# Gates of batch 0 in one Softplus pass, masks first, later v loads and a new written-out order in a gated linear attention with an MLP mixer

## Chip, cores and metric

The kernel runs on one core of a Trainium2 chip. The metric is the device time of one execution in microseconds (us); the median of several executions counts. Engines: PE (TensorE, matrix products), DVE (VectorE), ACT (ScalarE), POOL (GpSimd), SP (SyncE, here only for DMA), and 16 DMA engines that serve all queues.

## What is computed

```python
f = 1.0 / (1.0 + np.exp(-f_logit))              # B, H, S, D = 4, 8, 768, 48
for t in range(S):
    state = f[:, :, t, :, None] * state + np.einsum('bhd,bhe->bhde', k[:, :, t], v[:, :, t])
    y[:, :, t] = np.einsum('bhd,bhde->bhe', q[:, :, t], state)
x = y.transpose(0, 2, 1, 3).reshape(B, S, H * D)        # 768 x 384 for each batch
h = np.maximum(x.transpose(0, 2, 1) @ w_tok1, 0.0) @ w_tok2
u = x + h.transpose(0, 2, 1)
out = u + np.maximum(u @ w_ch1, 0.0) @ w_ch2
```

## The kernel before

**Attention.** A batch is worked in three chunk pairs, P 0 to 2, each of 256 steps: two chunks of 128 partitions in all, two steps (j) for each partition. For a pair, ACT makes the negative logarithm of the gate from f in place, ln(1 + exp(-f)), in two passes over 128x768 (`gates`, L449 with Exp and L451 with Ln). The pair sum `two` adds the two steps (L444, by the helper `both`); PE multiplies it with the triangular matrix `tri` to running sums (L473; for later batches L475 and L476 in bf16) and, in batch 0, with `ones` to chunk totals (L480, into the same bank of PSUM). `first` (DVE, L502) takes the second step off. From sums and `first` ACT makes the decays GG with four Exp passes (L505, L522) and the totals' decay `glast` (L508; L512 for later batches, moved by a DMA, L518). DVE multiplies q and k with them (L444, tile qk, one product for each j). PE turns the result over `ident` (L550; two PSUM banks), ACT and DVE copy it out as qT and kT (L430, L432); in batches 2 and 3 the DMA does the turn (L535). Then come the scores (L585), masked to AmT by DVE (L628), or by ACT and POOL in four cases of batch 0 (L623, L625); the states' sums (L603), scaled by `glast` (L637) and copied to `state_bd`; and the outputs y from AmT and v (L669) and from q and the state (L661). y goes to x_bf and x_nat.

**Mixer.** tok1 (L713) and, after Relu to h1T, tok2 (L729) work over the steps; u_bf takes y plus the result, is turned (L770; by DMA, L759, for late batches) to uT. ch1 (L788) makes 2 x 12 groups of three products, evacuated by Relu to zT (ACT L439, DVE L441). ch2 (L807) adds twelve products for a tile of 128 rows; DVE adds u (L813), SP stores it (L706). The last tile of the last batch is split in 288 and 96 columns.

**What sets the order.** Nothing runs as it is written: `add` notes each operation with what it needs and makes, and `Plan.best` goes through a written-out list, `ORDER`, in which each number names an operation (by 4) and its choice of engine (mod 4). A model of costs (`cost`, `SLOTS`, `HELD`) gives each a start, and the operations are issued sorted by these starts. So each engine has a fixed order, and engines and queues work strictly in it. Where the model sees PE idle, it sets **empty products** (`idle`, L848: 128x512 over a constant tile, `steady`, that nothing reads). The model's numbers are no times of this profile.

**Loads.** f of batch 0 comes over SP and ACT, all other loads over POOL's queue; a load of POOL waits until the eighth before it has landed.

Of the kernel before, what the change touches and what calls it, by code (L numbers as in the profile page):

```python
# [79 lines left out]
)  # L80
KEPT = 3
EARLY = ()
SPLIT = ()
MASKED = ((0, 0, 1), (1, 0, 1), (1, 1, 1), (2, 0, 1))
SLOTS = (6000, 7500, 10200, 11300, 12500, 13700, 14800, 16000, 17100, 20100, 21900)
HELD = (4300, 4300, 7100)


class Op:
# [167 lines left out]
def kernel(  # L257
# [25 lines left out]
    def st(shape, dtype, tag):  # L283
        return sb.tile(shape, dtype, tag=tag, name=tag)
# [597 lines left out]
```

## Time and profile before

| | |
|---|---|
| three runs | 168.51, 168.56, 169.04 us (median 168.56) |
| profiled execution | 168.51 us, span 166.8 us from the first to the last instruction |
| busy | PE 158.5, DVE 129.3, ACT 106.0, POOL 63.5 us |
| empty products | 32, 10.3 us of PE's busy time |
| chain that ended last | PE 75%, ACT 13%, DVE 5% of the span |
| moved | HBM read 25.17 MB, written 4.72 MB |

A row of the timeline gives start and length in us, engine, line, operation, output<-inputs, shapes and xcount; in brackets stands the idle time of the engine before it, and what ended it. "issue" means that it waited for nothing that the profile shows. A q behind the engine's name is its queue. A row of DMA issues gives the count, the size and the time from issue to landing.

### The profile page before, as it was taken

The numbers are of one execution on the slowest core, as the hardware profiler recorded it, in microseconds if no ns is written. First come the engines' busy times: TensorE is split into PE (matmuls) and PEld (weight loads), VectorE is DVE, ScalarE is ACT, GpSimd is POOL, SyncE is SP. The second block draws the span as 40 slices with busy tenths as digits, with TensorE's granted clock in tenths as the row PEclk, the third lists the DMA queues.
The fourth block names the chain that finished last, engine by engine and source line by source line (L and its number), as shares of the span: only waits on it lengthen the run. The fifth ranks groups of instructions, "written<-read, shape, count | busy, mean of one in ns | idle before, by whom it ended". The sixth has DMA issues, their size and how long they took to land.

```text
span 166.8 us, 5023 instructions
## 1 busy us (share of the span) xinstructions
PE 158.5 (95%) x2064; PEld 101.5 (61%) x2064; DVE 129.3 (78%) x287; ACT 106.0 (64%) x228; POOL 63.5 (38%) x87
## 2 busy tenths in 40 slices
PE   5899997899999999999999999999999999999991
PEld 2467865656666666566665766665667566566660
DVE  3499995889899998999999998996699446460331
ACT  3788975789899999976957939386531311725000
POOL 7975899705877200675517003024022022000000
PEclk9999999999999999999999999999999999999998
DMA  5999999999999991599999660985730043600253
GB/s 122 220 177 171 202 211 238 190 233 217 207 221 217 224 238 27 77 162 198 198 199 141 125 165 0 106 158 118 185 120 4 0 98 81 205 0 4 78 194 105
DMA packets 68183, 24.34 MB, mean 146 GB/s; under 512 B 60896, under 2 KB 67296, under 8 KB 68160
## 3 DMA queue, kind: packets, MB, share of 16 engines
q0 software_dynamic: 41856, 13.77, 67.6%
q1 hardware_dynamic: 25776, 10.06, 28.2%
q8 instruction: 16, 0.26, 0.6%
q10 hardware_dynamic: 528, 0.20, 0.4%
q14 instruction: 7, 0.06, 0.1%
HBM read 25.17 MB, written 4.72 MB: 179 GB/s over the span
## 4 chain that ended last, share of the span: by engine, by line
PE 75%; ACT 13%; DVE 5%; issue 2%; DMA 2%; DVEq 0%; ACTq 0%
PE ps L788 27%; PE ps L807 22%; PE ps L729 4%; PE ps L713 4%; PE ps L585 3%; PE ps L669 3%; ACT state_bd L430 2%; PE ps L661 2%; DMA f_sb<-in_f_logit_dram 2%; PE ps L603 2%; ACT f_sb L449 2%; ACT GG L522 2%; PE ps L550 2%; ACT f_sb L451 2%; ACT GG L505 1%
## 5 line engine op out<-in xcount | busy, mean ns | idle before, releaser
L807 PE MATMUL ps<-w_ch,zT 128*128 128x384 bf16 (+2 forms) x300 | 52.1, 320 | 0.4 <-ACT x_nat L430 0.4
L788 PE MATMUL ps<-uT,w_ch 128*128 128x384 bf16 x288 | 50.3, 326 | 0.1
L807 PEld LDWEIGHTS <-zT 128*128 128x128 bf16 x300 | 28.2, 98 | 17.7 <-issue 0.4
L788 PEld LDWEIGHTS <-w_ch 128*128 128x128 bf16 x288 | 27.7, 98 | 17.9 <-issue 0.3
L439 ACT ACTIVATE zT<-ps 128x384 bf16<-128x384 f32 x58 | 26.0, 495 | 16.9 <-PE ps L788 16.7
L628 DVE TENSOR_TENSOR AmT<-ps,mask 128x512 bf16<-128x512 f32 x44 | 28.3, 680 | 1.0 <-PE ps L585 0.8
L441 DVE TENSOR_SCALAR zT<-ps 128x384 bf16<-128x384 f32 x38 | 20.0, 552 | 6.1 <-PE ps L788 6.0
L813 DVE TENSOR_TENSOR x_nat<-x_nat,ps 128x384 f32<-128x384 f32 (+2 forms) x25 | 13.0, 532 | 10.3 <-PE ps L807 10.3
L434 POOL CAST state_bd<-state 48x192 bf16<-48x192 f32 x16 | 5.9, 369 | 33.0 <-DVE state L645 24.3
L444 DVE TENSOR_TENSOR qk<-qk_sb,GG 128x768 bf16<-128x768 bf16 x24 | 13.9, 585 | 1.2 <-ACT GG L522 1.1
L745 DVE TENSOR_TENSOR x_nat<-x_nat,ps 128x384 f32<-128x384 f32 x21 | 10.6, 548 | 3.9 <-PE ps L729 3.9
L358 POOL DMA_DIRECT2D v_sb<-in_v_dram x12 | 10.7, 888 | 5.7 <-DMA w_ch<-in_moe_w_ch_dram 4.9
L505 ACT ACTIVATE GG<-ps 128x384 bf16<-128x384 f32 x24 | 10.8, 488 | 3.1 <-DVE first L502 1.4
L522 ACT ACTIVATE GG<-first 128x384 bf16<-128x384 f32 x24 | 11.8, 520 | 0.6 <-DVE first L502 0.4
L449 ACT ACTIVATE f_sb<-f_sb 128x768 f32<-128x768 f32 x12 | 10.1, 845 | 2.9 <-DMA f_sb<-in_f_logit_dram 2.9
L848 PE MATMUL ps<-steady 128*128 128x512 bf16 x32 | 10.3, 444 | 1.7 <-DVE steady L373 1.7
L434 POOL COPY qT<-qJ 128x1024 bf16<-128x1024 bf16 x5 | 6.0, 1197 | 14.7 <-DMA qJ<-qk 14.6
L358 POOL DMA_DIRECT2D qk_sb<-in_k_dram x12 | 10.8, 900 | 2.0 <-POOLq L866 0.8
L430 ACT ACTIVATE u_bf<-x_nat 128x384 bf16<-128x384 f32 x13 | 6.0, 528 | 8.0 <-DVE x_nat L745 8.0
L358 POOL DMA_DIRECT2D qk_sb<-in_q_dram x12 | 10.6, 887 | 1.3 <-DMA qk_sb<-in_q_dram 0.7
L430 ACT ACTIVATE x_bf<-ps 128x384 bf16<-128x384 f32 x13 | 6.3, 490 | 6.2 <-PE ps L669 4.4
L713 PE MATMUL ps<-x_bf,w_tok 128*128 128x384 bf16 x48 | 10.1, 326 | 0.1
(84 smaller groups left out, 227.8 us busy)
## 6 DMA issues: line engine op xcount, KB each, us to landing
out_dram<-x_nat SPq DMA_DIRECT2D x23, 192.0 KB, 2.2
f_sb<-in_f_logit_dram POOLq DMA_DIRECT2D x9, 384.0 KB, 8.6
qk_sb<-in_k_dram POOLq DMA_DIRECT2D x12, 192.0 KB, 8.7
qk_sb<-in_q_dram POOLq DMA_DIRECT2D x12, 192.0 KB, 8.7
v_sb<-in_v_dram POOLq DMA_DIRECT2D x12, 192.0 KB, 8.8
w_ch<-in_moe_w_ch_dram POOLq DMA_DIRECT2D x2, 576.0 KB, 13.9
w_ch<-in_moe_w_ch_dram POOLq DMA_DIRECT2D x1, 1152.0 KB, 13.1
f_sb<-in_f_logit_dram SPq DMA_DIRECT2D x2, 384.0 KB, 5.6
```

Of the source, the lines that this page charges most:

```text
L358: lambda eng=eng, into=held(dst[i], P), of=runs(src, b, P): eng.dma_start(out=into, in_=of),
L430: nc.scalar.activation(out_, in_, AF.Copy, bias=0.0, scale=1.0)
L439: nc.scalar.activation(out_, in_, AF.Relu, bias=0.0, scale=1.0)
L441: nc.vector.tensor_scalar(out_, in_, 0.0, None, ALU.max)
L444: (nc.vector if op.engine == DVE else nc.gpsimd).tensor_tensor(out_, a, b_, what)
L449: add(ACT, r, lambda: nc.scalar.activation(fb, fb, AF.Exp, bias=0.0, scale=-1.0), make=[key], kind=el, need=([("fb", P)] if P < 1 else []) ...
L522: add(ACT, r, lambda n=n: nc.scalar.activation(GG[i][:, 0, n], banks[p_f.at][:, 0:DM].rearrange("t (h d) -> t h d", d=D) if split else fir ...
L628: add(DVE, r, lambda into=into, made=made, m4=m4: nc.vector.tensor_tensor(into, made(), m4, ALU.mult), need=masks, make=[("AmT", i, js, pa ...
L713: add(PE, rank("tok1", rt), lambda rt=rt, kt=kt, pm=pm: nc.tensor.matmul(banks[pm.at][:, 0:DM], lhsT=w_tok1[:, kt, rt * 128:(rt + 1) * 128 ...
L788: nc.tensor.matmul(banks[pm.at][:, 0:384], lhsT=w[:, kt, c0:c0 + 128], rhs=uT[:, th, :, kt, :], start=(kt == 0), stop=(kt == 2))
L807: nc.tensor.matmul(banks[pm.at][:, 0:n1 - n0], lhsT=zT[:, kt, tt * 128:(tt + 1) * 128], rhs=w_ch2[:, kt, n0:n1], start=(kt == 0), stop=(kt ...
L813: add(DVE, rank("ch2", tt), lambda un=un, pm=pm, n=n1 - n0: nc.vector.tensor_tensor(un, un, banks[pm.at][:, 0:n], ALU.add), make=[("x_nat" ...
```

## The change

1. **One pass.** In P 0 and P 1 of batch 0 (`SOFT`) the gate is one ACTIVATE with Softplus. ACT starts with the table set "softplus" and loads the one with Exp and Ln behind these two passes; everything of batch 0 that uses Exp waits for it ("tables").
2. **Masks first.** DVE sets all constants in one operation at the start (`constants`), and the first pair sum waits for `ident` and `tri2`. `steady` is a single column now, read as a broadcast. `tri_less` and two unused variants go.
3. **Totals of P 0** go to the bank of the states (p_st) instead of that of the sums.
4. **Loads.** v of P 1 stands behind q and k of P 2 (`LOADS`).
5. **Empty products** get margins: fewer are set into a gap.
6. **Costs** of the model are changed, the last tile's 288 columns go ahead of its 96 (`closing`), and `ORDER` is new as a whole, with other choices of engine.

The new numbering of lines is that of the diff; products with `steady` go from 32 to 22. Three places show what moves. Names carry the number of the buffer (GG_82 and GG_83 are the two decay tiles of even and odd pairs).

ACT, from its first pass on, before (batch 0: passes of P 0 and P 1, decays, then P 2):

```order
L449 ACTIVATE f_sb_74<-f_sb_74 128x8x96
L451 ACTIVATE f_sb_74<-f_sb_74 128x8x96
L449 ACTIVATE f_sb_74<-f_sb_74 128x8x96
L451 ACTIVATE f_sb_74<-f_sb_74 128x8x96
L505 ACTIVATE GG_82<-ps_121 128x384 x2
L522 ACTIVATE GG_82<-first_80 128x384 x2
L508 ACTIVATE glast_94<-ps_121 128x4x2
L505 ACTIVATE GG_83<-ps_122 128x384
L449 ACTIVATE f_sb_74<-f_sb_74 128x8x96
L451 ACTIVATE f_sb_74<-f_sb_74 128x8x96
L430 ACTIVATE qT_86<-ps_124 128x1024
L505 ACTIVATE GG_83<-ps_122 128x384
```

After:

```order
L452 ACTIVATE f_sb_74<-f_sb_74 128x8x96 x2
L839 ACT_TABLE_LOAD
L500 ACTIVATE GG_82<-ps_120 128x384
L517 ACTIVATE GG_82<-first_80 128x384 x2
L500 ACTIVATE GG_82<-ps_120 128x384
L500 ACTIVATE GG_83<-ps_121 128x384 x2
L503 ACTIVATE glast_94<-ps_122 128x4x2
L455 ACTIVATE f_sb_74<-f_sb_74 128x8x96
L432 ACTIVATE qT_86<-ps_123 128x1024
L457 ACTIVATE f_sb_74<-f_sb_74 128x8x96
L503 ACTIVATE glast_95<-ps_121 128x4x2
L517 ACTIVATE GG_83<-first_81 128x384 x2
```

Two passes stand where four stood, a table load behind them; the second decays of P 1 now stand ahead of Exp of P 2 and of qT.

DVE at the mixer of batch 0, before, from the second half of h1T to the third copy to uT:

```order
L441 TENSOR_SCALAR h1T<-ps_122 128x384
L432 CAST u_bf<-ps_127 128x384
L745 TENSOR_TENSOR u_bf<-x_nat_104,ps_121 128x384
L745 TENSOR_TENSOR u_bf<-x_nat_104,ps_123 128x384
L745 TENSOR_TENSOR u_bf<-x_nat_104,ps_128 128x384
L432 COPY uT<-ps_125 128x3x128
L745 TENSOR_TENSOR x_nat_104<-x_nat_104,ps_123 128x384
L432 COPY uT<-ps_126 128x3x128
L745 TENSOR_TENSOR x_nat_104<-x_nat_104,ps_121 128x384
L432 COPY uT<-ps_125 128x3x128
```

After, from the first copy to u_bf at the same place:

```order
L434 CAST u_bf<-ps_120 128x384
L739 TENSOR_TENSOR u_bf<-x_nat_104,ps_121 128x384
L434 COPY uT<-ps_127 128x3x128
L434 COPY uT<-ps_125 128x3x128
L434 COPY x_nat_104<-ps_124 128x384
L739 TENSOR_TENSOR u_bf<-x_nat_104,ps_126 128x384
L739 TENSOR_TENSOR u_bf<-x_nat_104,ps_122 128x384
L739 TENSOR_TENSOR x_nat_104<-x_nat_104,ps_126 128x384
L739 TENSOR_TENSOR x_nat_104<-x_nat_104,ps_122 128x384
L446 TENSOR_TENSOR two_77<-f_sb_75 128x8x48
L739 TENSOR_TENSOR x_nat_104<-x_nat_104,ps_121 128x384
```

h1T is ACT's alone, and uT copies stand ahead of two of the three sums to u_bf.

POOL's queue from its sixth load on (k, q and v of a pair are three rows; qk_sb_68 and v_sb_71 are batch 0's, 69 and 72 batch 1's), before:

```order
L358 DMA v_sb_71<-in_v_dram 128x8x96
L358 DMA qk_sb_68<-in_k_dram 128x8x96
L358 DMA qk_sb_68<-in_q_dram 128x8x96
L358 DMA v_sb_71<-in_v_dram 128x8x96
L403 DMA w_tok_63<-in_moe_w_tok_dram 128x6x256
L365 DMA w_tok_64<-in_moe_w_tok_dram 128x2x768
L365 DMA w_ch_65<-in_moe_w_ch_dram 128x3x768
L365 DMA w_ch_66<-in_moe_w_ch_dram 128x3x768
L358 DMA f_sb_75<-in_f_logit_dram 128x8x96
L625 TENSOR_TENSOR AmT_92<-AmT_92,mask 128x512
L358 DMA qk_sb_69<-in_k_dram 128x8x96
L358 DMA qk_sb_69<-in_q_dram 128x8x96
```

After, from the same load on:

```order
L356 DMA qk_sb_68<-in_k_dram 128x8x96
L446 TENSOR_TENSOR two_77<-f_sb_74 128x8x48
L356 DMA qk_sb_68<-in_q_dram 128x8x96
L356 DMA v_sb_71<-in_v_dram 128x8x96 x2
L416 DMA w_tok_63<-in_moe_w_tok_dram 128x6x256
L363 DMA w_tok_64<-in_moe_w_tok_dram 128x2x768
L363 DMA w_ch_65<-in_moe_w_ch_dram 128x3x768
L363 DMA w_ch_66<-in_moe_w_ch_dram 128x3x768
L446 TENSOR_TENSOR qk_85<-qk_sb_68,GG_83 128x2x8x48
L619 TENSOR_TENSOR AmT_92<-AmT_92,mask 128x512
L446 TENSOR_TENSOR qk_84<-qk_sb_68,GG_82 128x2x8x48
L356 DMA f_sb_75<-in_f_logit_dram 128x8x96
```

The pair sum of P 1 and one half each of the products with q and k of P 1 and P 2 have come to POOL from DVE, and batch 1's loads stand behind the last two.

The diff, cut to its core:

```diff
-    8, 12, 0, 20, 24, 28, 4, 16, 244, 248, 252, 256, 140, 32, 44, 48, 36, 168, 120, 124, 132, 172, 40, 268, 128,
...
+    0, 4, 12, 16, 8, 20, 24, 28, 32, 188, 192, 196, 80, 88, 92, 96, 100, 357, 104, 108, 48, 36, 40, 44, 52, 56,
...
-EARLY = ()
-SPLIT = ()
+SOFT = (0, 1)
+LOADS = (("v", 0), ("kq", 1), ("kq", 2), ("v", 1), ("v", 2))
-SLOTS = (6000, 7500, 10200, 11300, 12500, 13700, 14800, 16000, 17100, 20100, 21900)
-HELD = (4300, 4300, 7100)
+SLOTS = (6150, 7850, 10350, 11500, 12700, 13850, 15000, 16450, 17400, 19500, 21800)
+HELD = (3850, 4300, 7100)
...
-            if e == PE and free[PE] < until and t - free[PE] > 250:
-                n = int((t - free[PE] - 1000) / 430) if not free[PE] else int((t - free[PE] - 40) / 218)
+            if e == PE and free[PE] < until and t - free[PE] > 270:
+                n = int((t - free[PE] - 500) / 430) if not free[PE] else int((t - free[PE] - 50) / 215)
...
-    steady = st([128, 512], BF16, "steady")
+    steady = st([128, 1], BF16, "steady")
...
+    nc.vector.memset(steady, 1.0)
     nc.vector.memset(tri_bf, 1.0)
-    nc.vector.memset(steady, 1.0)
+
+    def constants():
+        nc.vector.memset(ones, 0.0)
...
+    once(DVE, constants, ["ones", "start"] + [(n, i) for n in ("two", "ends") for i in range(2)] + [("sbd", i) for i in range(3)]
+         + [("qk", i, j) for i in range(NQ) for j in range(2)], 2550)
...
-    once(ACT, lambda: nc.scalar.preload_act_table_set("natural_log_exp_and_others"), ["table"], 1280)
+    once(ACT, lambda: nc.scalar.preload_act_table_set("softplus" if SOFT else "natural_log_exp_and_others"), ["table"], 1280)
...
-    load("v", 0, 0)
-    load("kqv", 0, 1)
-    load("kqv", 0, 2)
+    for what, P in LOADS:
+        load(what, 0, P)
...
+        if b == 0 and P in SOFT:
+            add(ACT, r, lambda: nc.scalar.activation(fb, fb, AF.Softplus, bias=0.0, scale=-1.0), make=[key, ("soft", P)], kind=el,
+                need=["table"] + ([("fb", P)] if P < 1 else []))
+            return
...
-        op = add((DVE, POOL) if b == 0 else DVE, r, None, need=[key], make=[("two", i)], kind=("el", DM, False, 1.2))
+        op = add((DVE, POOL) if b == 0 else DVE, r, None, need=[key] + (["ident", "tri2"] if b + P == 0 else []), make=[("two", i)], kind=("el", DM, False, 1.2))
...
+        p_n = p_st if P == 0 else p_s
+        n0 = HP * D if P == 0 else DM
...
-                nc.tensor.matmul(banks[p_s.at][:, DM + 2 * hp:DM + 2 * hp + 2], lhsT=blk(two[i])[:, hp, :], rhs=ones,
-                                 start=True, stop=True)
...
+                nc.tensor.matmul(banks[p_n.at][:, n0 + 2 * hp:n0 + 2 * hp + 2], lhsT=blk(two[i])[:, hp, :], rhs=ones,
+                                 start=P > 0 or hp == 0, stop=True, skip_group_check=P == 0)
...
+                    if b == B - 1:
+                        if n0:
+                            plan.ops[-1].before.update(closing)
+                        else:
+                            closing.append(plan.ops[-1])
...
+            if b == 0 and P == len(SOFT):
+                once(ACT, lambda: nc.scalar.preload_act_table_set("natural_log_exp_and_others"), ["tables"], 1280 if SOFT else 10,
+                     ["table"] + [("soft", p) for p in SOFT])
...
-            nc.tensor.matmul(banks[NBANK - 1], lhsT=steady[:, 0:128], rhs=steady, start=True, stop=True)
+            nc.tensor.matmul(banks[NBANK - 1], lhsT=steady.broadcast_to((128, 128)), rhs=steady.broadcast_to((128, 512)), start=True, stop=True)
```

More of the change, by code (lines that the diff above doesn't have):

```diff
@@ L162, in cost @@
         if what == "el":
-            free, psum, fast = n
+            free, psum, fast, *more = n
             if engine == ACT:
@@ L167, in cost @@
             if engine == DVE:
-                own = free / (0.96 * int(fast)) + 67
-                return own, own + 83
+                own = free / (0.96 * int(fast)) + 67 + sum(more)
+                return own, own + 83 - sum(more)
             own = free * (2.05 if fast % 1 else 1.2) + 80
@@ L464, in sums_and_turns @@
         p_s = Bank()
-        early, split = b == 0 and P in EARLY, b == 0 and P in SPLIT
+        p_n = p_st if P == 0 else p_s
+        n0 = HP * D if P == 0 else DM
         def sums():
             pm = banks[p_s.at][:, 0:DM]
-            if early:
-                for j in range(2):
-                    nc.tensor.matmul(pm, lhsT=tri, rhs=fb[:, :, j], start=j == 0, stop=j == 1)
-            elif b == 0:
+            if b == 0:
                 nc.tensor.matmul(pm, lhsT=tri, rhs=two[i][:, :, 0:D], start=True, stop=True)
@@ L609, in attention @@
         if b:
-            chain = add(PE, r, lambda: parts(range(live)), need=have, bank=p_d[0], kind=("mm", 450 if live > 1 else 260), tail_of=chain)
+            chain = add(PE, r, lambda: parts(range(live)), need=have, bank=p_d[0], kind=("mm", 352), tail_of=chain)
             plan.maker[p_d[live - 1]] = chain
@@ L635, in attention @@
             if b == 0:
-                add(PE, r, lambda x=x: parts([x]), need=have, make=["sums"], bank=p_st, kind=("mm", 300))
+                add(PE, r, lambda x=x: parts([x]), need=have, make=["sums"], bank=p_st, kind=("mm", 365))
                 add(DVE, r, lambda x=x, gb=gb: nc.vector.tensor_tensor(dg(x), dg(x), gb, ALU.mult),
@@ L683, in attention @@
         lead = add(PE, r, lambda: None, need=ready, bank=p_y[0], kind=("mm", 1), room=2)
[L684 removed]
+        lead = add(PE, r, outs, need=ready, bank=p_y[1], kind=("mm", 775 if P else 510), tail_of=lead)
         plan.maker[p_y[0]] = lead
[L686 removed]
+        add(PE, r, lambda: before(1, False), need=past(1), bank=p_y[1], kind=("mm", 200))
         for x in range(2):
```

85 lines of the change are left out of this document (36 added, 49 removed), and 109 rows, old and new, of the table ORDER.

## Prediction

> **What bounds the kernel now.** I read the page first, then the table by stretches of 10 us.
>
> ```profile
> PE   5899997899999999999999999999999999999991
> ...
> PEclk9999999999999999999999999999999999999998
> ...
> L848 PE MATMUL ps<-steady 128*128 128x512 bf16 x32 | 10.3, 444 | 1.7 <-DVE steady L373 1.7
> ...
> 30.00:40.00 10.00, 9.57 (x72) 6.06 (x70) 9.20 (x21) 9.31 (x22) 4.17 (x6) 1.00 1.52 214
> 40.00:50.00 10.00, 10.00 (x143) 6.85 (x142) 9.44 (x20) 9.47 (x20) 7.55 (x9) 1.00 1.84 215
> 50.00:60.00 10.00, 9.57 (x191) 6.70 (x190) 9.80 (x22) 9.98 (x22) 4.42 (x6) 1.00 1.81 225
> 60.00:70.00 10.00, 9.81 (x138) 6.17 (x137) 9.51 (x21) 9.83 (x24) 1.61 (x2) 1.00 0.54 91
> ```
>
> The first two rows of digits cut the span in 40 slices (busy share and granted clock, in tenths). In the stretches, behind the bounds and the length, stand the busy times of PE, PEld, DVE, ACT and POOL. From 32 us on, PE is busy almost without a break; between 30 and 70 its idle time is 0.43 + 0.43 + 0.19 us. So behind the start **TensorE is the bound**: the same products take the same time in whatever order, and only what comes ahead of that stage and behind it can shrink. Ahead of it PE only looks busy: 32 empty products (L848, 10.3 us) fill its waits. There the chain runs f, gates, decays, products with q and k, turns, scores, three chunk pairs one behind the other, and then the mixer of batch 0. PE becomes the bound with the first ch1 product at 32.77. So the time is about: start of ch1, plus PE's remaining work, plus the tail. From 40 to 70 ACT is just as full (29.3 of 30 us), which makes the first rival.
>
> **The start.** Rows of the opening, in order of time:
>
> ```profile
> 1.32 1.28 ACT L376 ACT_TABLE_LOAD   x1 [1.32 <-PEq L866]
> ...
> 4.43 0.84 ACT L449 ACTIVATE f_sb<-f_sb 128x768 f32<-128x768 f32 x1 [1.82 <-DMA f_sb<-in_f_logit_dram]
> ...
> 3.30 0.31 POOL L380 TENSOR_SCALAR_AFFINE_SELECT tri_bf<-tri_bf 128x128 bf16<-128x128 bf16 x1
> ...
> 6.21 0.90 POOL L358 DMA_DIRECT2D v_sb<-in_v_dram  x1
> ...
> 6.79 0.91 PE L473 MATMUL ps<-two,tri 128*128 128x384 f32 x2 [0.43 <-DVE two L444]
> ...
> 7.54 0.95 PE L480 MATMUL ps<-ones,two 128*128 128x2 f32 x8
> ...
> 8.53 0.56 DVE L502 TENSOR_TENSOR first<-ps,f_sb 128x384 f32<-128x384 f32 x1 [0.18 <-PE ps L480]
> ...
> 9.12 0.87 ACT L505 ACTIVATE GG<-ps 128x384 bf16<-128x384 f32 x2 [1.37 <-DVE first L502]
> ...
> 9.87 0.94 ACT L522 ACTIVATE GG<-first 128x384 bf16<-128x384 f32 x2
> ...
> 11.32 0.49 DVE L444 TENSOR_TENSOR qk<-qk_sb,GG 128x768 bf16<-128x768 bf16 x1
> ...
> 12.23 1.07 PE L550 MATMUL ps<-ident,qk 128*128 128x128 bf16 x16
> ...
> f_sb<-in_f_logit_dram SPq DMA_DIRECT2D x1, 384.0 KB, 4.2
> ```
>
> Before, f of P 0 takes two ACT passes (L449, L451), and `first` waits until 8.53 for the totals (L480), since they write the bank that it reads. After, one pass is enough: 4.43 + 0.84 = 5.27. Then the pair sum (0.56, as `first`) and the sums (0.91): 6.8. The second pass can't start before f of P 1 has landed (the last row: issued at 1.35, 4.2 us later, 5.6), so it ends at 6.46, and the new table load (1.28) at 7.75. The decays need table and sums: 7.77, against 9.12. Four of them took 1.69 (9.12 to 10.81), so they end at 9.46, and the products with q and k (0.55 each) at 10.2, against 11.81. Now PE is late: the pair sum of P 1 is on POOL, behind its sixth load, so it starts at about 7.1 (where the sixth, L358 of v, ends now). No row shows it there; by elements from POOL's own product below (1.27 for 512) it takes 0.95, bounded by DVE's 0.56 and by 1.27. I take 0.9: 8.0. Sums (0.75 till the next starts), two totals (0.8 each) and an empty product follow: the turns start at 10.65, a **gain of 1.6 us** over 12.23.
>
> It does not last:
>
> ```profile
> 14.63 0.48 PEld L585 LDWEIGHTS <-kT 48*64 48x64 bf16 x32 [0.27 <-DVE kT L432]
> ...
> 16.30 0.55 DVE L444 TENSOR_TENSOR qk<-qk_sb,GG 128x768 bf16<-128x768 bf16 x1
> ...
> 16.59 1.27 POOL L625 TENSOR_TENSOR AmT<-AmT,mask 128x512 bf16<-128x512 bf16 x1 [0.93 <-ACT AmT L623]
> ...
> 19.55 0.71 PE L585 MATMUL ps<-qT,kT 48*64 48x128 bf16 x32
> ...
> 22.68 0.64 PE L585 MATMUL ps<-qT,kT 48*64 48x128 bf16 x32
> ```
>
> *Scores of P 0*: on ACT, qT stands behind the decay of the totals (which end at 10.5) and Exp of P 2 (0.84), so it starts at 11.6; with 1.02 for itself the scores come at 12.7 against 14.63, gain 1.9. *P 1*: half of the product with q and k is now POOL's. From 512 elements in 1.27 its 768 take 1.7 to 1.9 (bounds: DVE's 0.55, and 1.9), and it waits for the last decays, which stand on ACT behind qT and Ln of P 2 and end at 14.4 (11.6 + 0.9 + 0.9 + 0.94, by starts): 14.4 to 16.2, against 16.85. Then ACT's order has two state copies ahead of qT: scores at 18.85, against 19.55, gain 0.7. *P 2*: DVE's half waits for the decays from `first`, 19.6; turns at 20.25, and qT, behind an AmT copy, x_nat and two state copies, ends at 22.66: scores at 22.7, **no gain** over 22.68. The passes saved on ACT return as waits for the next chunk's decays; the three products that went to POOL spare DVE 3 x 0.55, which is not what ends last there.
>
> **The mixer of batch 0.**
>
> ```profile
> 26.02 0.32 PE L669 MATMUL ps<-v_sb,AmT 64*128 64x48 bf16 x11 [1.09 <-issue]
> ...
> 28.61 0.49 ACT L439 ACTIVATE h1T<-ps 128x384 bf16<-128x384 f32 x1 [0.51 <-PE ps L713]
> ...
> 29.10 0.56 DVE L441 TENSOR_SCALAR h1T<-ps 128x384 bf16<-128x384 f32 x1 [1.04 <-PE ps L713]
> ...
> 30.07 0.87 ACT L430 ACTIVATE u_bf<-ps 128x384 bf16<-128x384 f32 x2 [0.97 <-PE ps L729]
> ...
> 31.17 0.67 PE L770 MATMUL ps<-ident,u_bf 128*128 128x128 bf16 x9
> ...
> 32.12 0.35 DVE L432 COPY uT<-ps 128x384 bf16<-128x384 bf16 x1
> ...
> 32.26 0.68 PE L770 MATMUL ps<-ident,u_bf 128*128 128x128 bf16 x9 [0.43 <-DVE u_bf L745]
> ...
> 32.77 1.46 PE L788 MATMUL ps<-uT,w_ch 128*128 128x384 bf16 x8
> ...
> q8 instruction: 16, 0.26, 0.6%
> ```
>
> PE stands for 1.09 us in the middle of L669 and waits for nothing that the profile shows. Page part 3 has 16 packets of 16 KB on the instruction queue; I read this wait as such a block that came late. PE's 20 rows less move the place by ten products, to the end of the same group, and the block is asked for some 0.4 us earlier, since the scores of P 1 end earlier by that and more: the wait ends at 25.6. The Trainium skill, Runtime: NRT & Kernel Launch, section Instruction fetch mechanics, says that the instructions come in blocks of 16 KiB and that the cost of crossing into the next one is mostly hidden; by that the sum would be the one of the last rival below. The row of L669 shows 1.09 us that were not hidden.
>
> From there: eight L661 and P 2's 32 L669 end at 26.5, a copy of y on DVE (0.56) at 27.4, and the last two tok1 products (0.163 each, and some 0.2 to the end) at 28.0, where h1T starts (28.61). Both halves are ACT's, so the second ends at 28.9 instead of 29.66. The sixth tok2 product, with which three tiles are ready, ends at 29.5, ACT's two u_bf (0.87) at 30.3, and nine transposes start there (31.17). ch1 stands behind these nine alone; before, it stood behind 18, with 0.43 of waiting between. The uT copies (0.35 on DVE, the last behind the ninth transpose) are covered in part by two tok2 products, so ch1 starts at **31.1, 1.67 earlier**. Nine transposes (0.67 busy, 0.5 on PE's queue) are only moved behind it. Net gain: 1.67 - 0.50 = 1.17.
>
> **The tail.**
>
> ```profile
> 156.65 0.25 DVE L813 TENSOR_TENSOR x_nat<-x_nat,ps 128x96 f32<-128x96 f32 x1 [1.77 <-PE ps L807]
> ...
> 163.22 0.55 DVE L813 TENSOR_TENSOR x_nat<-x_nat,ps 128x384 f32<-128x384 f32 x1 [0.78 <-PE ps L807]
> ...
> out_dram<-x_nat SPq DMA_DIRECT2D x1, 192.0 KB, 1.9
> out_dram<-x_nat SPq DMA_DIRECT2D x1, 48.0 KB, 1.5
> ```
>
> The last tile is now the one of 96 columns: behind PE's last product stand 0.25 instead of 0.55, and a store that lands 1.5 instead of 1.9 us behind its issue (the row with 192 KB is the last store alone). The full tile ahead of it ends at almost the same time (its sum is free 12 short products earlier, and its store is longer), so I count 0.55 of these 0.7.
>
> **Sum**, from the profiled execution's 168.51 (span 166.8, 1.7 around it; the median of the runs is 168.56): 168.51 - 1.17 - 0.55 = 166.8. At nothing I cost, first, the masks ahead of the first pair sum, which now waits for two of them: DVE's five small copies follow POOL's select (3.61) and end by about 4.8, 0.5 ahead of f's pass, and even a later sum is covered until the table has come at 7.75. Then v behind q: scores need q and k alone. Then `steady` in one column: 11 empty products at their mean of 0.444 end at 6.0, where the sums begin, and 0.9 us more would be covered by the table load. Last, the loads behind POOL's products:
>
> ```profile
> 25.27 1.06 POOL L365 DMA_DIRECT2D w_ch<-in_moe_w_ch_dram  x1
> ...
> w_ch<-in_moe_w_ch_dram POOLq DMA_DIRECT2D x1, 1152.0 KB, 13.1
> ```
>
> w_ch2 lands at 38.4. After, it is issued some 2 us later, but it lands when the loads ahead of it have passed, and the first ch2 product stands behind 51 ch1 products (0.163 each, from 8 in 1.46 less the last's end) and a few turns: about 40. Later than that, each microsecond would be one of PE's.
>
> **Rivals.** *ACT gives the gain back.* In 40 to 70 ACT has 0.72 us to spare, and the same evacuations are asked for some 1.2 us earlier. For it: 9.98 of 10. Against it: PE waited only 0.43 for all that. Then the tail alone remains, and half a microsecond of the front at most: 168.0, around the border between faster and the same (about 0.3%, 0.5 us, is what a measurement of this kernel can tell from no change).
>
> *Slower, by the same place:* ACT's queue is in order. If the new order sets one chunk of batch 1 so that PE meets its scores before ACT has passed four decays (1.69) and qT (0.92), PE stands for 2.6 us: 169.4. It decides from 2.3 us of such waits on. PE's order is wholly new from ch1 on, with the first ch2 products some 200 rows earlier; this speaks for it.
>
> *The clock falls back.* Empty products go from 32 to 22, and between 5 and 13 us PE will be idle for about 2 us in pieces of 0.4 to 1. The granted clock is 9 or more in every slice but the last, and the pause of 1.09 us did not change it; but no row shows so thin a stretch of 8 us. At half the clock, what PE does for P 0 until its turns end (two sums 1.5, totals 1.6, turns 0.9) takes 4 us more on the path: 170.8. It decides from 2.3 us on. A one-column operand that feeds PE more slowly would end here too.
>
> *The table change costs more.* The first load took 1.28, but nothing was under way ahead of it. If the same 1.28 is paid once more behind the passes of P 0 and P 1, decays start at 9.05; the turns, then bound by ACT, at 11.6, and ch1 some 0.9 later: 167.7. The Trainium skill, ScalarE: Activation LUTs, section What ACT_TABLE_LOAD costs, gives 1283 ns for the load and 1380 ns of drain, 2.66 us for each switch. By it this case would come out 0.1 us later than priced here. The first load's row agrees with the 1283 ns; no row shows a drain, since ACT was idle ahead of it.
>
> *The block wait is gone.* If the block comes in time, the group of P 2 behind it waits for DVE's last AmT instead, ready at about 25.1, and PE gains 0.8 us: 166.0. Against it: loads fill the queues at that place as before.
>
> **How the numbers follow.** Forecast (166.1 to 167.5) 0.45; no block wait 0.12; dearer table 0.06; ACT gives back 0.17 (0.07 of it faster, 0.10 the same); a chunk of batch 1 late 0.13; clock 0.07. Faster: 0.45 + 0.12 + 0.06 + 0.07 = 0.70; the same 0.10; slower 0.20. The likeliest gives 166.8. The range goes from the case without the block wait and 0.6 us less of waiting in the full stage (of the 1.05 us of idle time between 30 and 70) to the late chunk: 165.4 to 169.4.
>
> **What will show it.** In the changed profile: a second table load of 1.28 that ends near 7.75, decays at 7.8, turns of P 0 at 10.65; scores near 12.7, 18.9 and 22.7; a wait of PE without a releaser near 24.6 to 25.6; ch1 near 31.1; PE idle by no more than some 1 us between there and the last product; a last row of 96 columns on DVE. If scores of P 2 come before 22, the loss on ACT was overrated; if ch1 is early and the time is not, one of the first two rivals holds, and PE's waits for ACT between 40 and 70 name the row. The prediction is wrong if PE's idle time behind ch1 grows by over 1 us, or if ch1 comes later than 32.

## The result, and the profile after

The changed kernel takes **167.01 us** (median of 20 runs, 166.45 to 171.42), the kernel before 168.61 in the same comparison: a ratio of 0.9906, 95% interval 0.9882 to 0.993. Ratios here and below leave out runs that took over 1.5% longer than the fastest run of their kernel. The forecast was 166.8. The profiled execution took 167.46, 1.05 less than the 168.51 of before. First its two rows of digits, busy share of PE and granted clock:

```profile
PE   7599989999999999999999999979999999999991
...
PEclk9987999999999999999999999999999999999998
```

The third and fourth slice (8 to 17 us) show a lower clock, which the kernel before did not have: the trace records it as half from 11.13 us on, for 3.41 us. The opening in order of time (start, duration, engine, line):

```profile
5.98 0.91 PE L477 MATMUL ps<-two,tri 128*128 128x384 f32 x2 [0.81 <-DVE two L446]
...
6.51 1.28 ACT L839 ACT_TABLE_LOAD   x1
...
7.10 1.03 POOL L446 TENSOR_TENSOR two<-f_sb 128x384 f32<-128x384 f32 x1
7.80 0.49 ACT L500 ACTIVATE GG<-ps 128x384 bf16<-128x384 f32 x1
8.19 0.91 PE L477 MATMUL ps<-two,tri 128*128 128x384 f32 x2 [0.86 <-POOL two L446]
...
10.85 1.65 PE L544 MATMUL ps<-ident,qk 128*128 128x128 bf16 x16
...
13.95 0.90 PE L579 MATMUL ps<-qT,kT 48*64 48x128 bf16 x32
...
14.41 1.64 POOL L446 TENSOR_TENSOR qk<-qk_sb,GG 128x768 bf16<-128x768 bf16 x1
```

Decays stand at 7.80 (7.77 was forecast), turns of P 0 at 10.85 (10.65). But these 16 turns take 1.65 in place of the 1.07 of before: PE works at half its clock here, and scores of P 0 come at 13.95, not 12.7. Then the mixer of batch 0:

```profile
25.92 0.20 PE L663 MATMUL ps<-v_sb,AmT 64*128 64x48 bf16 x2 [0.30 <-issue]
...
28.38 0.98 ACT L441 ACTIVATE h1T<-ps 128x384 bf16<-128x384 f32 x2 [0.68 <-PE ps L707]
...
29.77 0.87 ACT L432 ACTIVATE u_bf<-ps 128x384 bf16<-128x384 f32 x2 [0.41 <-PE ps L723]
...
30.55 0.71 PE L764 MATMUL ps<-ident,u_bf 128*128 128x128 bf16 x9
...
31.67 2.60 PE L782 MATMUL ps<-uT,w_ch 128*128 128x384 bf16 x15
```

The wait without a releaser has moved to the end of its group, two products before it, and shrunk from 1.09 to 0.30. ch1 starts at 31.67, 1.10 earlier than before. Behind it, in stretches of 10 us (PE's busy time is the second number):

```profile
50.00:60.00 10.00, 10.00 (x216) 6.70 (x215) 9.88 (x22) 9.80 (x22) 7.91 (x9) 1.00 1.75 229
60.00:70.00 10.00, 9.99 (x133) 6.46 (x130) 9.69 (x23) 9.90 (x25) 0.00 (x0) 1.00 1.48 216
...
100.00:110.00 10.00, 9.31 (x116) 5.50 (x114) 9.82 (x21) 5.54 (x14) 3.19 (x5) 1.00 0.80 93
```

ACT is as full as before, and PE waits for nothing there. But at 109 a wait has come that before had not. From PE's rows, and from the chain that ended last, where the transfer waited for stands with its start and length:

```profile
110.17 2.12 PE L782 MATMUL ps<-uT,w_ch 128*128 128x384 bf16 x12 [0.87 <-DMA uT<-u_bf]
```

```profile
104.70 5.43 DMA uT<-u_bf
```

Last the tail. Stretches of 1 us, of before and of the changed kernel; the last two numbers are the mean busy share of the DMA engines and GB/s:

```profile
162.00:163.00 1.00, 1.00 (x8) 0.49 (x5) 0.45 (x1) 0.00 (x0) 0.00 (x0) 1.00 0.55 197
163.00:164.00 1.00, 0.18 (x2) 0.00 (x0) 0.55 (x1) 0.00 (x0) 0.00 (x0) 1.00 0.46 148
```

```profile
162.00:163.00 1.00, 0.20 (x5) 0.05 (x2) 0.49 (x2) 0.00 (x0) 0.00 (x0) 1.00 1.01 344
163.00:164.00 1.00, 0.00 (x0) 0.00 (x0) 0.00 (x0) 0.00 (x0) 0.00 (x0) 1.00 1.01 354
```

Before, PE's last product ended at 163.18 and the last store landed at 165.65; now these are 162.20 and 164.60. So the tail went from 2.47 to 2.40: the last row is short, but the DMA engines are full with the stores ahead of it. The 1.05 us are thus: start of ch1 -1.10, from ch1 to PE's last product +0.12 (130.41 before, 130.53 after), tail -0.07.

### The profile page after: what moved, and what is told of

Same layout as the page of the kernel before. It is cut to its first block, busy times and chain, and to the rows that moved or that the text cites. A ratio compares the mean times of both kernels' runs of the same rounds, so it can differ in the third digit from the quotient of the medians.

```text
span 165.8 us, 4994 instructions
## 1 busy us (share of the span) xinstructions
PE 157.5 (95%) x2054; PEld 101.1 (61%) x2054; DVE 127.9 (77%) x284; ACT 107.9 (65%) x229; POOL 64.8 (39%) x87
## 4 chain that ended last, share of the span: by engine, by line
PE 76%; DMA 3%; ACT 2%; DVE 2%; issue 0%; SPq 0%
PE ps L801 27%; PE ps L782 27%; PE ps L707 5%; PE ps L663 3%; PE ps L723 3%; DMA uT<-u_bf 3%; PE ps L579 3%; PE ps L655 2%; PE ps L544 2%; PE ps L764 1%; PE ps L597 1%; PE ps L479 1%; DVE x_nat L739 1%; DVE x_nat L812 1%; PE ps L480 1%; ACT u_bf L432 1%
## 5 line engine op out<-in xcount | busy, mean ns | idle before, releaser
L782 PE MATMUL ps<-uT,w_ch 128*128 128x384 bf16 x288 | 49.6, 326 | 1.0 <-DMA uT<-u_bf 0.9
L441 ACT ACTIVATE zT<-ps 128x384 bf16<-128x384 f32 x57 | 25.6, 503 | 18.1 <-PE ps L782 17.9
L436 POOL COPY qT<-qJ 128x1024 bf16<-128x1024 bf16 x3 | 3.5, 1150 | 27.1 <-PE ps L597 17.8
L446 DVE TENSOR_TENSOR qk<-qk_sb,GG 128x768 bf16<-128x768 bf16 x22 | 12.0, 553 | 1.8 <-ACT GG L517 1.5
L500 ACT ACTIVATE GG<-ps 128x384 bf16<-128x384 f32 x24 | 11.4, 486 | 1.6 <-PE ps L484 1.5
L432 ACT ACTIVATE x_nat<-ps 128x384 f32<-128x384 f32 x15 | 7.2, 488 | 6.8 <-PE ps L663 6.8
L723 PE MATMUL ps<-h1T,w_tok 128*128 128x384 bf16 x48 | 9.4, 326 | 0.1
L356 POOL DMA_DIRECT2D f_sb<-in_f_logit_dram x9 | 8.2, 911 | 2.3 <-DVE qk L446 0.9
```

The source lines that it names most:

```text
L356: lambda eng=eng, into=held(dst[i], P), of=runs(src, b, P): eng.dma_start(out=into, in_=of),
L432: nc.scalar.activation(out_, in_, AF.Copy, bias=0.0, scale=1.0)
L441: nc.scalar.activation(out_, in_, AF.Relu, bias=0.0, scale=1.0)
L446: (nc.vector if op.engine == DVE else nc.gpsimd).tensor_tensor(out_, a, b_, what)
L723: nc.tensor.matmul(banks[pm.at][:, 0:DM], lhsT=w_tok2[:, kt, tt * 128:(tt + 1) * 128], rhs=h1T[:, kt, :], start=(kt == 0 and not held), st ...
L782: nc.tensor.matmul(banks[pm.at][:, 0:384], lhsT=w[:, kt, c0:c0 + 128], rhs=uT[:, th, :, kt, :], start=(kt == 0), stop=(kt == 2))
```

## The experiments

Medians of all runs of each kernel, and the ratio to the runs of the kernel before that were taken beside it; their medians go from 168.60 to 168.91, so small differences between two lines of the table are uncertain by some 0.3 us. The clock of a run is the mean granted clock. "Low" counts the runs with a clock of 0.99 or less, out of all. One fall to half the clock for 3.41 us, as above, takes 0.5 x 3.41 / 166 = 0.010 off that mean.

| kernel | us, median (range) | ratio, 95% | low |
|---|---|---|---|
| changed | 167.01 (166.45-171.42) | 0.9906 (0.9882-0.9930) | 7 of 20 |
| x_fill | 166.90 (166.20-167.28) | 0.9881 (0.9836-0.9925) | 0 of 6 |
| x_wide | 166.79 (166.55-170.04) | 0.9888 (0.9841-0.9935) | 1 of 6 |
| x_thin | 170.61 (170.31-175.82) | 1.0102 (1.0065-1.0139) | 2 of 6 |
| x_two_pass | 168.04 (167.48-168.72) | 0.9953 (0.9932-0.9974) | 0 of 12 |
| x_extra | 167.35 (167.22-168.83) | 0.9932 (0.9900-0.9963) | 2 of 8 |
| b_soft | 168.35 (167.60-168.99) | 0.9975 (0.9951-0.9999) | 0 of 12 |
| b_soft2 | 170.87 (169.36-172.05) | 1.0109 (1.0074-1.0143) | 9 of 12 |
| x_tail | 167.58 (166.73-168.87) | 0.9926 (0.9890-0.9963) | 5 of 12 |
| x_vlate | 165.50 (165.28-166.66) | 0.9812 (0.9769-0.9854) | 1 of 6 |
| x_both_act | 165.63 (165.11-166.52) | 0.9812 (0.9777-0.9847) | 1 of 6 |
| x_best | 166.12 (165.14-170.31) | 0.9803 (0.9758-0.9849) | 3 of 6 |
| x_last | 165.86 (165.26-167.01) | 0.9836 (0.9792-0.9879) | 2 of 6 |

**The clock.** x_fill closes the two thin places of the opening:

```
+                n += 2 if not free[PE] else 4 if free[PE] < 7000 else 0
                 fill = Op((PE,), 0.0, lambda n=n: idle(n), ...
```

> The changed kernel with six more empty products: two more in the first stretch, and four more ahead of the sums of P 1, where its profile shows PE idle for 0.81 us (5.17 to 5.98) and 0.86 us (7.33 to 8.19). Theory (these two thin places let the clock fall back from about 10 to 15 us, and that costs the runs with a granted clock under 1.00): every run has a clock of 1.00, PE's turns of P 0 take 1.07 and not 1.65 us, the median is 166.6, no run is over 167.2. Rival 1 (the clock falls for another reason, as the one-column operand): clocks of 0.98 to 1.00 as before, median 167.0. Rival 2 (the six products are in the way): median over 167.2. The wait of PE in front of a product with v and no releaser moves by twelve rows, six products, to an earlier place if it is a block of instructions that comes late.

```profile
1.00 5.73 PE L851 MATMUL ps<-steady 128*128 128x512 bf16 x13 [1.00 <-DVE steady L371]
...
11.08 1.05 PE L545 MATMUL ps<-ident,qk 128*128 128x128 bf16 x16
...
12.97 0.64 PE L580 MATMUL ps<-qT,kT 48*64 48x128 bf16 x32
```

All six clocks are 0.995 or more and the turns take 1.05, as the theory said. The same empty products in x_extra and x_both_act, below, have low runs again (2 of 8, 1 of 6), so the falls are rarer and not gone. The median is hardly lower, 166.90 where 166.6 was expected, and one run took 167.28. In this profile the empty products ran at half speed throughout (13 in 5.73), so the first sums waited for them until 6.52, against 5.98. The wait in front of a product with v, which was expected to move, is gone (nothing over 0.15 us).

x_wide gives them a full operand:

```
-    steady = st([128, 1], BF16, "steady")
+    steady = st([128, 512], BF16, "steady")
...
-            nc.tensor.matmul(..., lhsT=steady.broadcast_to((128, 128)), rhs=steady.broadcast_to((128, 512)), ...
+            nc.tensor.matmul(..., lhsT=steady[:, 0:128], rhs=steady, ...
```

> The changed kernel with a full operand for the empty products (128 x 512 numbers in place of one column that is read again and again). Theory (width of the operand does not matter for the clock): granted clocks of 0.98 to 1.00 as in the changed kernel, median 167.0, mean of one empty product 0.44 us in the opening as with one column. Rival (one column feeds PE more thinly, and the clock falls for that): all clocks 1.00 and the median 166.6.

```profile
1.53 4.88 PE L850 MATMUL ps<-steady 128*128 128x512 bf16 x11 [1.53 <-DVE steady L370]
```

One low run in six, against seven in 20, does not tell the two apart. The products start 0.53 later, behind a longer memset, and take 0.44 each, as in x_fill. With the full operand a run is low too, and x_fill holds the clock with one column: nothing here speaks for the column as the cause, but that it plays no part is not shown. x_thin goes the other way:

```
+                n -= 3 if not free[PE] else 2 if free[PE] < 7000 else 0
```

> The changed kernel with five empty products less in the opening: eight in the first stretch in place of eleven, and none ahead of the sums of P 1 in place of two, so that PE is idle there for some 1.5 and 1.4 us (0.81 and 0.86 before). Theory (these two thin places let the clock fall back): the granted clock is 0.99 or lower in every run, PE works at half the clock for 5 us or more from about 8 us on, first ch1 product at 31.7 or later, median 167.8 to 169.0. Rival (the clock falls in some runs whatever PE does in the opening): clocks spread as in the changed kernel, 1.00 in two thirds of the runs, median 167.0.

```profile
5.77 1.65 PE L478 MATMUL ps<-two,tri 128*128 128x384 f32 x2 [1.17 <-DVE two L447]
...
9.65 3.41 PE L485 MATMUL ps<-ones,two 128*128 128x2 f32 x16
...
13.30 1.91 PE L545 MATMUL ps<-ident,qk 128*128 128x128 bf16 x16
```

Five empty products less cost 3.6 us. The expectation on the clock's number failed: four runs show 0.996 to 1.00, so the mean clock doesn't tell of this; the products do. In this trace the record of the clock begins at 16.64, where PE comes up to speed, and what lies ahead counts as full. The products take 1.8 times as long from the first sums to about 16 us: PE had not come up to speed before its first pause.

**Softplus and the table.** x_two_pass puts Exp and Ln into each of the two operations of Softplus and drops the second load:

```
+            def passes():
+                nc.scalar.activation(fb, fb, AF.Exp, bias=0.0, scale=-1.0)
+                nc.scalar.activation(fb, fb, AF.Ln, bias=1.0, scale=1.0)
...
-    once(ACT, lambda: nc.scalar.preload_act_table_set("natural_log_exp_and_others"), ["tables"], ...
+    once(ACT, lambda: None, ["tables"], ...
...
+                n += 6 if not free[PE] else 6 if free[PE] < 7000 else 0
```

> The changed kernel with Exp and Ln in the place of each of its two Softplus passes, one table for all of them (the second table load goes), and with ten to twelve empty products more in the opening so that the clock holds; the order is the changed one. To be compared with the changed kernel with six more empty products (166.9, first ch1 product at 30.6). Theory (one pass is worth what it saves on the chain to the turns of P 0, and the table load takes most of it back on ACT): decays of P 0 start at about 7.9 as with Softplus (two passes of 0.84 more, one load of 1.28 less), but f of P 1 is ready 1.4 us later, its sums start at 8.95, turns of P 0 at about 11.7 against 11.1; ch1 is 0.4 to 0.8 later and the time 167.3 to 167.7. Rival 1 (Softplus alone makes the gain, and the order nothing): 168.5. Rival 2 (the gain of one pass is lost at P 1 and P 2, where ACT is full): 166.9.

```profile
7.93 1.01 POOL L447 TENSOR_TENSOR two<-f_sb 128x384 f32<-128x384 f32 x1 [0.82 <-ACT f_sb L455]
...
8.43 0.49 ACT L505 ACTIVATE GG<-ps 128x384 bf16<-128x384 f32 x1 [0.58 <-DVE first L502]
...
9.38 0.81 PE L482 MATMUL ps<-two,tri 128*128 128x384 f32 x2
...
11.94 1.05 PE L549 MATMUL ps<-ident,qk 128*128 128x128 bf16 x16
```

The first decays of x_fill, to compare:

```profile
8.00 0.49 ACT L501 ACTIVATE GG<-ps 128x384 bf16<-128x384 f32 x1 [0.40 <-DVE first L498]
```

Decays come 0.4 later than there, sums of P 1 at 9.38 (0.44 behind POOL's end, since empty products stand there), turns at 11.94 against 11.08, ch1 at 31.61 against 30.68. The median is 1.1 higher, more than expected, the profiled run 0.7; up to 0.4 of that are the empty products. So one pass is worth 0.7 to 1.1, about half of the gain, and it comes by the sums of P 1 above all, which stand ahead of the turns on PE. No run divides the other half among POOL's products, the totals' bank and the order. x_extra loads one more table in the same place:

```
-    once(ACT, lambda: nc.scalar.preload_act_table_set("natural_log_exp_and_others"), ["tables"], ...
+    once(ACT, lambda: [nc.scalar.preload_act_table_set(n) for n in ("exp_and_others", "natural_log_exp_and_others")], ["tables"], ...
```

> The changed kernel with six more empty products, and with a third table load in front of the second one, which nothing needs. Theory (a table load costs its own 1.28 us, no drain; the decays are on the path to ch1): the two loads take 2.56 from 6.3 to 8.9, the next pass follows within 0.1 us, decays of P 0 at 9.3 against 8.0; turns of P 0, which wait 0.6 for PE otherwise, come 0.7 later, scores of P 2 and ch1 0.7 to 1.28 later, time 167.6 to 168.2 against 166.9. Rival 1 (a switch drains ACT for 1.38 us more each time): a pause of over 1 us stands between a load and the next pass, and the time is over 169. Rival 2 (a delay of the decays is lost again before ch1): 166.9 to 167.2.

```profile
6.46 2.57 ACT L840 ACT_TABLE_LOAD   x2
9.04 0.49 ACT L501 ACTIVATE GG<-ps 128x384 bf16<-128x384 f32 x1
```

Two loads take 2.57, the next pass follows 0.01 later: a load costs its 1.28 and no more. The Trainium skill, ScalarE: Activation LUTs, section What ACT_TABLE_LOAD costs, adds 1380 ns of drain to each switch; here no drain stands in the rows. Of the 1.28 only 0.45 reach the end by the medians (0.9 by the two ratios), less than expected, since the turns still start at 11.08: PE, not the table, is late there. In the profiles ch1 comes 0.25 later (30.93 against 30.68), and 0.16 come from a longer wait for uT (1.43 at 110 us, against 1.27).

b_soft puts Softplus and the second load into the kernel before, with one empty product less:

```
+        soft = b == 0 and P < 2
-        add(ACT, r, lambda: nc.scalar.activation(fb, fb, AF.Exp, ...
+        add(ACT, r, lambda: nc.scalar.activation(fb, fb, AF.Softplus if soft else AF.Exp, ...
...
+            (lambda: nc.scalar.preload_act_table_set("natural_log_exp_and_others") if P else None), ...
```

> The kernel before with Softplus alone: one pass in place of Exp and Ln for batch 0, P 0 and P 1, the second table load behind them, one empty product less at the start; the order is that of before. Theory (what f gains goes on along the chain to ch1): f of P 0 0.84 earlier, decays at 8.3 against 9.12, turns of P 0 at 11.4 against 12.23, ch1 0.4 to 0.84 earlier than 32.77, time 167.8 to 168.2 against 168.6. Rival 1 (the load takes it all back): 168.6. Rival 2 (Softplus alone is the whole change): 167.0.

```profile
2.50 4.47 PE L851 MATMUL ps<-steady 128*128 128x512 bf16 x10
...
6.77 1.14 PE L476 MATMUL ps<-two,tri 128*128 128x384 f32 x2
```

The first row has the last ten of the twelve empty products. This tells little: at half speed they last until 6.97, the sums start when they did before, and ch1 at 32.75 (32.77 before). The median is 0.3 lower, at the edge of what the interval tells from nothing. b_soft2 leaves out more:

```
-                n -= 1 if not free[PE] else 0
+                n -= 4 if not free[PE] else 2 if 9000 < free[PE] < 10000 else 0
```

> The kernel before with Softplus alone once more, now with so many empty products less (four at the start, two ahead of the turns of P 0) that none stands in the way of the sums, as they did with one less (there they ended at 6.97, and decays came at 9.32). Theory: sums of P 0 at 6.0 against 6.79, decays at 8.3 to 8.5 against 9.12, turns of P 0 at 11.4 to 11.6 against 12.23, ch1 at 32.0 to 32.5 against 32.77, time 167.8 to 168.2 against 168.6: Softplus alone is under half of the gain, since taking it out of the changed kernel cost 1.1. Rival 1 (Softplus alone gives nothing with the order of before): 168.6. Rival 2 (Softplus alone is the whole change): 167.0.

```profile
20.10 0.32 PE L588 MATMUL ps<-qT,kT 48*64 48x128 bf16 x9 [0.80 <-issue]
...
27.01 0.24 PE L672 MATMUL ps<-v_sb,AmT 64*128 64x48 bf16 x5 [1.83 <-issue]
```

The chain runs as expected up to here (decays 8.55, turns 11.42, scores of P 0 at 13.83), and so do the scores of P 1 (18.73 against 19.55); then everything is lost. PE waits 0.80 and 1.83 us for instructions, 128 products apart, where before had one wait of 1.09; behind the second its clock falls by half for 3.4 us, and ch1 comes at 34.93. So in this run the earlier start bought only longer waits for blocks. Whether that lies in the order of before is not shown: the edit took six empty products out as well, which moves each block's border by six products, and nine of the twelve runs have a low clock.

**The tail.** x_tail sets the short tile one place ahead of the last full one:

```
-    3120, 4060, 4080, 4020, 4040, 3972, 4084, 4088, 4092, 3976, 4096, 3980, 4100,
+    3120, 4060, 4080, 4020, 4040, 4084, 4088, 4092, 4096, 4100, 3972, 3976, 3980,
...
-                            plan.ops[-1].before.update(closing)
+                            pass
```

> The changed kernel with the last tile's 96 columns one place ahead of the last 384 columns, so that the last row on DVE is a full one again. As the prediction had it, a last row of 96 columns is worth 0.55 us: then this kernel is 0.55 us slower than the changed one, 167.55, and its store lands about 3 us behind DVE's last start. Theory now (SP is issuing stores one behind the other, 0.4 to 0.5 us each, up to 162.86, so that the short last row waits 0.37 us for SP and its store lands 164.60, 2.40 us behind PE's last product, against 2.45 before the change): within 0.15 us of the changed kernel, 167.0 to 167.15.

By its median this is unclear, since 5 of its 12 runs have a low clock; the other seven have a median of 166.91, against 166.81 for the same runs of the changed kernel. By its profile, the tail is 2.59 us against 2.40. So the place of the short tile is worth 0.1 to 0.2, not 0.55.

**The wait at 109.** x_vlate moves one load (number 1712 of the order) on POOL's queue:

```
-    3264, 3372, 1712, 2840, ...
+    ... 2912, 2917, 3392, 1712, 3280, ...
```

> The changed kernel with one load (v of batch 3, P 2) moved on POOL's queue from behind u_bf of batch 2 (issued at 103.56, landed at 109.24) to behind the next copy of qT (about 113). Theory (this load shares the DMA queues with the second transposing DMA of u_bf, which takes 5.43 us in place of 3.2 and holds ch1 of batch 2 up for 0.87 us at 109.3): the transposing DMA lands 2 us earlier, PE's wait at 109.3 is gone, the median falls by 0.8 us to 166.2. Rival 1 (the transposing DMA takes 5.4 us for its own reasons, behind the first one and the qJ transposes): wait and time stay, 167.0. Rival 2 (later on the load comes in the way of qJ and kT of batch 3): the wait moves there, 166.6 to 167.5.

```profile
105.98 6.34 PE L782 MATMUL ps<-uT,w_ch 128*128 128x384 bf16 x38
```

The two transposing DMAs to uT, issue to landing (median of both), in the changed kernel and here:

```profile
uT<-u_bf SPq DMA_TRANSPOSE x2, 4.3
```

```profile
uT<-u_bf SPq DMA_TRANSPOSE x2, 3.8
```

The wait is gone (38 products in one piece), the second transposing DMA lands 4.35 behind its issue in place of 5.43 (the first takes 3.2 in both, so the load accounts for half of the second one's extra 2.2; the rest is open), and PE needs 129.49 from ch1 to its last product in place of 130.53. This kernel beats the one before and the changed one: 165.5, ratio 0.9812 (0.9769 to 0.9854), 0.7 lower than expected. All seven profiles of the new order with the load in its old place have this wait, 0.87 to 1.43 us long; the four with the load moved have none. The load's place cost 1.0 to 1.4 us.

**Put together.** x_both_act adds to x_fill the load's place, as in x_vlate, and the last two stores on ACT's queue:

```
+        (nc.scalar if last else nc.sync).dma_start(out=to, in_=un)
```

> The changed kernel with three edits: six more empty products in the opening, the load of v of batch 3, P 2 behind the next copy of qT, and the last two stores (tile 0 and the last 96 columns) issued by ACT in place of SP. Theory: clocks of 0.995 to 1.00 in every run; no wait of PE at 108 to 109; the tail from PE's last product to the last landing falls from 2.38 to about 2.15, since the last row's store no longer waits for SP; median 165.1 to 165.4, against 166.9 with the empty products alone and 165.5 with the load alone. Rival (the extra empty products cost on the path what they give to the clock): 165.6 to 165.9.

165.63, which is what the rival expected; one run of six is low, and the tail stays at 2.40. x_best has the load's place, three empty products more in the second thin place only, and one store on ACT:

```
+                n += 3 if 6000 < free[PE] < 7000 else 0
...
+        (nc.scalar if far else nc.sync).dma_start(out=to, in_=un)
```

> The changed kernel with the load of v of batch 3, P 2 behind the next copy of qT, three more empty products in the second thin place alone (ahead of the sums of P 1, where they fit into 0.86 us of waiting), and the store of tile 0 on ACT's queue, so that the last 96 columns find SP's free. Theory: clocks of 0.995 to 1.00, first ch1 product at 30.5, no wait of PE at 108, tail of 2.2 in place of 2.4; median 165.0 to 165.3. Rival 1 (one thin place of 0.8 us is enough to let the clock fall): some runs at 0.99 or lower and 166 or more. Rival 2 (SP's queue does not hold the last store up): tail 2.4, median 165.4.

```profile
160.00:161.00 1.00, 0.00 (x0) 0.00 (x0) 0.18 (x1) 0.00 (x0) 0.00 (x0) 1.00 1.02 359
161.00:162.00 1.00, 0.00 (x0) 0.00 (x0) 0.00 (x0) 0.00 (x0) 0.00 (x0) 1.00 0.82 274
```

The last store is issued 0.03 behind its row now, but lands 2.08 later in place of 1.74; the tail is 2.39 as in the others. So SP's queue, my theory in three expectations, does not set the tail: the DMA engines are full then (1.02 and 0.82 of their time). Three runs of six have a low clock: the second place alone does not do it. x_last adds one product in the first stretch:

```
-                n += 3 if 6000 < free[PE] < 7000 else 0
+                n += 1 if not free[PE] else 3 if 6000 < free[PE] < 7000 else 0
```

> The changed kernel with the load of v of batch 3, P 2 moved behind the next copy of qT, one empty product more in the first stretch and three more ahead of the sums of P 1, and the store of tile 0 on ACT's queue. Theory (the two thin places together cool the clock; where the first ends late enough, none is left): median 165.2, at most one run in six with a clock under 0.995, no wait of PE at 108. Rival (what is added in front of the first sums delays them in runs whose products stay at half speed until about 6 us): ch1 0.1 to 0.2 later than 30.4, median 165.4 to 165.6. The tail from PE's last product to the last landing stays 2.4, as it did with the store on ACT alone.

```profile
10.00:15.00 5.00, 5.00 (x75) 3.59 (x76) 3.09 (x9) 4.44 (x10) 4.39 (x6) 0.66 2.02 171
```

Two runs of six are low, where one at most was expected, and the median is 165.86, not 165.2. In the profiled one PE was idle for 0.28 and 0.48 us alone in the two thin places, and the clock fell all the same. "The two thin places" is therefore not the whole cause.

## Why the prediction was right, and where it was not

Time and sign were right, the time in part by luck: three of its terms, the start of ch1, the time from there to the last product, and the tail, were wrong and cancelled. The second column of numbers is the profiled run of the changed kernel, the third that of x_wide, the same program but for the empty products' operand, with a clock that held.

| step | forecast | changed | x_wide |
|---|---|---|---|
| turns of P 0 | 10.65 | 10.85 | 10.87 |
| scores P 0, P 1, P 2 | 12.7, 18.85, 22.7 | 13.95, 19.66, 23.61 | 12.75, 18.63, 22.59 |
| wait for the block, and its end | 1.0, 25.6 | 0.30, 25.92 | 0.18, 24.77 |
| start of ch1 | 31.1 | 31.67 | 30.52 |
| ch1 to the last product, against before | +0.5 | +0.12 | +0.36 |
| tail, against before | -0.55 | -0.07 | -0.09 |
| time | 166.8 | 167.46 | 166.55 |

- *One pass, sums on POOL, second load:* right within 0.2 us, and so is the loss by P 2, with scores at 22.59 where 22.7 was forecast. The "dearer table" was mispriced: its 1.28 was to cost 0.9, x_extra measured 0.45 by the medians, 0.25 of it at ch1.
- *The block wait:* the place was right within a product or two, the end was not. I had the block asked for 0.4 us earlier; x_wide has it 1.25 earlier than before (24.77 against 26.02). This term was too dear by 0.8, and ch1 came 0.6 earlier than forecast in x_wide, and 0.2 to 0.7 earlier in x_both_act, x_fill and x_best (30.90, 30.68, 30.38), whose clock held too. *The block wait is gone*, given 0.12, was the nearer case there: 0.18 us of the wait is left in x_wide, 0.22 in x_both_act, nothing over 0.15 in x_fill and x_best.
- *Nine transposes behind ch1, +0.5:* not seen. They do stand there (27 against 18), but PE's busy time behind the start of ch1 is 129.69 before and 129.66 after, and its idle time there 0.72 and 0.87; what became shorter by 0.5 is open. Of the 1.05 us of idle time that I counted in the full stage, some 0.3 lie ahead of ch1, so less was to be had there.
- *The tail:* failed. Priced at 0.55 from one DVE row and one landing; measured 0.07 to 0.09. The stores of the last tiles now stand in the DMA engines one behind the other (busy share 1.01 from 162 to 164 us, 0.55 and 0.46 before).
- *ACT gives the gain back:* did not happen (PE idle 0.01 us from 40 to 70, ACT 9.90 of 10). *A chunk of batch 1 late:* no. But the sign it stood for, a new wait in the full stage, came elsewhere: 0.87 us at 109, from a load beside a transposing DMA. I had looked at POOL's moved loads only as far as w_ch2 (which landed at 38.9, ahead of its use). x_vlate shows this one to be the cause.
- *The clock falls back:* given 0.07 at a price of 4 us, it came in 7 runs of 20, at a price of 0.7 to 2.4 us (167.46 to 169.25, against 166.81, the median of the other 13), with one at 171.42. The mechanism was there, at a lower price: I had the half clock last through all that PE does for P 0, and each fall in a trace lasts 3.41 us.

So the gain of 1.6 us is 1.8 where the clock holds (166.81 against 168.61), about half of it by Softplus (x_two_pass against x_fill), less what the clock takes in the other runs.

## What to carry to other kernels

Price a shorter last step by what is still in the DMA engines when it ends, and look at every transfer that a new order moves beside a transposing DMA that something waits for. An earlier chain on PE is worth only what the next instruction block and the clock leave of it: Softplus was worth about 1 us in the new order; put into the order of before, it gained 0.3 us with the empty products in its way, and with six of them left out the kernel lost 2.2 us. Empty products cost time when they are too many and more when they are too few, and how fast they run differs from run to run.

## What the runs showed of the hardware

**In four profiles the clock fell 6.83 us after it came up, for 3.41 us.** In the first stretch each empty product takes 0.43 us, later 0.22. In the profiles of the changed kernel, x_tail, x_vlate and x_last the record of the clock has this change at 3.8 to 4.4 us, and PE at half speed from 10.6 to 11.2 on, until 14.0 to 14.6. In nine other profiles the change came behind 5 us (in x_thin behind 15), and none of them fell between 10 and 15. x_two_pass, with 17 empty products, came up at 4.3 and did not fall. The Trainium skill, TensorE: Matmul & The Clock Gate, section What's actually happening, tells of a free-running window of 3413 ns; 6.83 is two of them, and that fits, as does b_soft2, which came up at 6.65 and fell 20.48 us later, six of them. The same page's section HAM oscillation warns of idle gaps over 3.4 us; here no gap ahead of the fall was over 1.1 us (1.83 in b_soft2). The runs show that more empty products make it rarer (3 low runs of 32 with 13 and more in the first stretch, 16 of 44 with eleven, x_wide apart). In those four profiles, the 3.41 us that end with the fall begin at 7.2 to 7.8, and so hold the end of the wait ahead of the sums of P 1 and nearly all the totals behind them; in x_wide, with the same products, a window ends at 6.37 + 3.41 = 9.78, in the middle of the totals. That the moment of coming up decides by this is an estimate from these rows; what is weighed within the window stays open.

**Instruction blocks follow PE.** In the trace a packet on the instruction queue starts 3.3 to 3.8 us behind the start of the block ahead (product 222 at 20.04, packet at 23.51 in the changed kernel; 4.6 in b_soft2), takes 0.89 to 0.97, and where PE waits for it, PE goes on 1.3 to 1.6 us behind its end. The 128 products from number 222 on take 5.5 to 6.2 us in all variants of the changed kernel; whether this part of the start could become shorter is not shown. Why b_soft2's second packet came 1.1 us later than that of before is open.
